# One program order for the whole first pass of a fused attention and gated-FFN kernel, and a shorter float64 rebuild

## Chip, cores and metric

The kernel runs on one core of one Trainium2 chip. The metric is device microseconds (us) of one execution, lower is better.

## Reference

Pooled attention over 8 batches, 8 heads, 576 positions and head size 64, followed by a gated feed-forward layer on the 4608 tokens. Everything is float32.

```python
def _attn_ref(q, k, v):
    k_p = k.reshape(B, H, Sp, pool, D).mean(axis=3)     # pool = 8, Sp = 72
    v_p = v.reshape(B, H, Sp, pool, D).mean(axis=3)
    scores = scale * np.matmul(q, k_p.transpose(0, 1, 3, 2))
    scores = scores - np.max(scores, axis=-1, keepdims=True)
    attn = np.exp(scores)
    attn = attn / (np.sum(attn, axis=-1, keepdims=True) + 1e-09)
    return np.matmul(attn, v_p)

def _moe_ref(x, w_gate, w_val, w_out):                  # 512 -> 1536 -> 512
    gate = 1.0 / (1.0 + np.exp(-(x @ w_gate)))
    return gate * (x @ w_val) @ w_out
```

The three weights arrive as float64; q, k and v as float32.

## The kernel before

The 4608 tokens are cut into 12 blocks of 384. A *pass* takes two blocks: pass n = 0 computes the feed-forward part of blocks 0 and 1, pass 1 that of blocks 2 and 3, up to pass 5. While a pass multiplies, the attention of the next two blocks runs between its products (`both`, `attention`), so pass 0 holds the attention of blocks 0, 1, 2 and 3.

Float32 products are made of three products of rounded parts: each operand is split into a high part (a copy by ACT into a 22-bit type, here called hi) and a low part (the difference, by DVE, lo). `xo` tiles are the parts of an attention result, `parts` those of a weight, `hs` those of the hidden layer, `oparts` those of `w_out`.

Pass 0 differs from the later ones. It has to rebuild each weight as float32 from the two 32-bit words of the float64 value (`to_f32`), split it (`converted`), keep the parts and the whole float32 weight in device memory (`keep`, `kept_w`; DMA issues named `keptG0A`, `keptwG` and so on), and use the parts at once in plain products (`whole`, 12 matmuls for one of G or V, one column group f and one block). There are 12 such weight pieces (G and V, p from 0 to 5; a piece gives f = 2p and 2p + 1). Later passes reload the kept parts and use a seven-product scheme (`product`), for which pass 1 makes sums of the whole weights (`add_up`, tile `w8`, and `sums`). The products of f = 8 to 11 for blocks 2 and 3 are still plain and open pass 1 (`hidden_second`, line 575 of the profile like those of pass 0).

Pass 0 before the change has three stages. `first_blocks` does the attention of blocks 0 and 1 and the first four products, in an order written out by hand (`manual_schedule`, line 1083) for PE, DVE, ACT and POOL. `hidden_first` does the other plain products, converts the remaining eight weight pieces and runs the attention of blocks 2 and 3 in between; its order comes from a scheduler. `second` rebuilds `w_out` (12 pieces, `convert_o`) and multiplies the hidden layer with it (line 717, tile `acc`). All loads and stores are issued by SP, in one queue.

`to_f32` takes one ACT instruction and four DVE instructions:

```python
pinned(nc.scalar.activation(w, hi.bitcast(F32), AF.Abs, scale=2.0 ** -112))             # L122, ACT
nc.vector.tensor_scalar(out=w, in0=w, scalar1=F64_MAX, ...op0=ALU.min)                   # L124, DVE
nc.vector.tensor_scalar(out=u, in0=u, scalar1=3, ...op0=ALU.logical_shift_left)          # L126, DVE
nc.vector.scalar_tensor_tensor(out=u, in0=hi, scalar=0x80000000, in1=u, ...)             # L128, DVE
nc.vector.scalar_tensor_tensor(out=u, in0=lo, scalar=29, in1=u, ...)                     # L132, DVE
```

Pooled v of batch 0 and of batch 1 is made by PE, as a product with a matrix of ones (`v_main`, line 1010, tile `vp`; `v_rest`, line 1020, tile `vr`); of the later batches by DVE reductions (`pool`, line 304, then `prep_v`).

Of the kernel before, what the change touches and what calls it, by code (L numbers as in the profile page):

```python
# [18 lines left out]
P = 128  # L19
# [41 lines left out]
def attention_then_ffn(ctx: ExitStack, tc: tile.TileContext, qT, kT, vm, vr, vn, sums8, wgv, wo, const, out, outT):  # L61
# [54 lines left out]
    words, parts, plain, oparts = {}, {}, {}, {}  # L116

    def to_f32(w, lo, hi):

        u = w.bitcast(U32)  # L120

        pinned(nc.scalar.activation(w, hi.bitcast(F32), AF.Abs, scale=2.0 ** -112))  # L122
# [12 lines left out]
        yield  # L135

    def fetch(kind, p):
        raw = big.tile([P, 4 * HALF, 2], U32, name="raw64", tag="big")
        nc.sync.dma_start(raw.rearrange("p n t -> p (n t)"), wgv[p, "GV".index(kind)].bitcast(U32))
        words[kind, p] = raw  # L140
# [11 lines left out]
    made = [0]  # L152

    def room_for_parts():

        made[0] += 1
        if made[0] <= 4 * NP and made[0] % 11 in (8, 9, 10):
            return work.tile([P, 2, 2, HALF], F32R, name="parts_x", tag=f"xo{(3, 6, 7)[made[0] % 11 - 8]}")
        return wpool.tile([P, 2, 2, HALF], F32R, name="parts", tag="parts")

    def converted(kind, p):
# [4 lines left out]
        w = (big if p else wpool).tile([P, 4, HALF], F32, name="w4", tag="big" if p else "parts")  # L166
        yield from to_f32(w.rearrange("p a n -> p (a n)"), raw[:, :, 0], raw[:, :, 1])
        for i, at in enumerate((slice(0, 4, 3), slice(1, 3))):
# [73 lines left out]
    def convert_o(f):  # L242
        raw = big.tile([P, 3 * DM], U32, name="raw_o", tag="big")
        nc.sync.dma_start(raw[:, :2 * DM], wo[f].bitcast(U32))
        pair = raw[:, :2 * DM].rearrange("p (n t) -> p n t", t=2)
        w = raw[:, 2 * DM:].bitcast(F32)
        for _ in to_f32(w, pair[:, :, 0], pair[:, :, 1]):
            pass
        t = opool.tile([P, 2, DM], F32R, name="oparts")
        split(t[:, 0], t[:, 1], w)  # L250
        nc.sync.dma_start(kept_o[f].rearrange("p h n -> p (h n)").bitcast(F32), t.rearrange("p h n -> p (h n)").bitcast(F32))
        for half in range(2):
# [3 lines left out]
        oparts[f] = t  # L256
# [97 lines left out]
    prepared, xs = {(0, 0), (0, 1)}, {}  # L354
# [17 lines left out]
    def rest_of(e, rz, copy):  # L372
# [11 lines left out]
        copy(r3v[2], restf)  # L384
        return r3

    def attention(j, g):
# [38 lines left out]
        r3 = rest_of(e, rz, nc.scalar.copy)  # L426
# [162 lines left out]

    def hidden_first(tasks):  # L590

        for p in range(1, NP + 1):
            if p in (2, 4):
                new_h(p // 2)
            for i in range(2):
                if p + 1 < NP:
                    steady[0] = p == 1
                    convert("GV"[i], p + 1)
                    steady[0] = False
                if 1 < p < NP:  # L600
# [97 lines left out]

    def second(tasks, build):
        order = ("b0", "b2", "b1", "b4", "b5", "b3")  # L700
        acc = {}
        for f in range(2):
            convert_o(f)
        for f in range(NF):
            if f + 2 < NF:
                convert_o(f + 2)
            hs = big.tile([P, 2, 2 * BT], F32R, name="hs", tag="big")
            hf = hb[f // 4][:, f % 4]
            nc.scalar.copy(hs[:, 0], hf)
            nc.vector.tensor_tensor(out=hs[:, 1], in0=hf, in1=hs[:, 0].bitcast(F32), op=ALU.subtract)  # L710
            o = oparts.pop(f)
            for i in range(2 * QT):
                if f == 0:
                    acc[i] = ps.tile([P, DM], F32, name="acc", tag=order[i])
                a = slice(i * P, (i + 1) * P)
                for k, (y, w) in enumerate(((0, 0), (1, 0), (0, 1))):
                    nc.tensor.matmul(  # L717
                        acc[i], lhsT=hs[:, y, a], rhs=o[:, w], start=(f == 0 and k == 0), stop=(f == NF - 1 and k == 2),
                    )
            if f < 5:  # L720
                next(tasks, None)
                next(tasks, None)
            elif f == 5:
                for _ in tasks:
                    pass
            else:
                next(build, None)
                if f == NF - 1:
                    next(build, None)
        for j in range(2):  # L730
            o = big.tile([P, QT, DM], F32, name="o", tag="big")
            for i in range(QT):
                store(o[:, i], j * BT + i * P, acc[j * QT + i], nc.vector if i % 2 else nc.scalar)
# [147 lines left out]
    def first_blocks():  # L881
# [304 lines left out]
```

## Time and profile before

| | us |
|---|---|
| median of 3 runs | 991.08 (989.36 to 992.35) |
| profiled execution, its own time | 990.34 |
| span of the profiled execution | 988.6 |

The time is that of one execution as the host sees the device; the span is from the first to the last instruction of the trace, and 1.7 us lie around it. Times in the trace count from the start of the span. PE is the matmul engine, DVE and ACT the two elementwise engines, POOL the general one, SP issues the DMAs. [...] A record (xN in the rows) is one instruction as the trace shows it; a float32 score matmul leaves two records.

### The profile page before, as it was taken

Reading aid. Unit: us, or ns where it says so; the run is one execution under the profiler, and the core shown is the slowest. Engines: PE = TensorE matmul, PEld = TensorE weight load, DVE = VectorE, ACT = ScalarE, POOL = GpSimd, SP = SyncE. Lnnn points to the kernel's source line nnn. Section 1 sums busy time; section 2 is a strip of 40 time slices with the busy share of each in tenths; the row PEclk is TensorE's granted clock in tenths of the full one; section 3 lists DMA queues with packets and bytes.
Section 4 is the critical chain, followed back from the end, with each engine's and each line's share of the span. In section 5 each row is a group of like instructions: output and inputs, shape, how many; then the busy total and the mean of one; then the engine's idle time right before and its main releaser. Section 6 shows DMA issues by size and latency. Waiting matters only on the chain.

```text
span 988.6 us, 15480 instructions
## 1 busy us (share of the span) xinstructions
PE 951.3 (96%) x5436; PEld 916.1 (93%) x5436; DVE 709.9 (72%) x1240; ACT 545.0 (55%) x1111; POOL 48.8 (5%) x67
## 2 busy tenths in 40 slices
PE   5779999999899999999999999999999999999998
PEld 4669999889899999998999999999999999999998
DVE  5867799885999789785598666689366669244474
ACT  4647677554576756655455456556355546233343
POOL 2010000000000000000000000000000000000000
PEclk8879999999999999999999999999999999999999
DMA  9736999678799578999558878747976637867567
GB/s 338 256 111 203 342 360 343 225 261 272 237 353 392 187 226 265 315 398 346 180 172 274 279 230 256 235 147 227 309 243 208 224 118 246 292 220 252 181 196 230
DMA packets 114861, 250.84 MB, mean 254 GB/s; under 512 B 11872, under 2 KB 49504, under 8 KB 113248
## 3 DMA queue, kind: packets, MB, share of 16 engines
q1 hardware_dynamic: 114784, 249.86, 75.0%
q8 instruction: 43, 0.70, 0.3%
q14 instruction: 34, 0.28, 0.1%
HBM read 193.19 MB, written 56.62 MB: 253 GB/s over the span
## 4 chain that ended last, share of the span: by engine, by line
PE 84%; DMA 6%; DVE 6%; ACT 3%; issue 1%; SPq 0%; DVEq 0%; ACTq 0%
PE chain L535 38%; PE acc L809 19%; PE chain L575 12%; PE acc L717 5%; PE sc L361 4%; PE av L370 3%; DMA out<-o 1%; PE tp L449 1%; PE vp L1010 1%; DVE s L741 1%; DVE hs L773 1%; DMA parts<-keptV2A 1%; DMA parts<-keptG4B 1%; DMA w<-keptwG 1%; DMA parts<-keptG1B 1%
## 5 line engine op out<-in xcount | busy, mean ns | idle before, releaser
L535 PE MATMUL chain<-xo,parts 128*128 128x384 f32 x2352 | 440.0, 340 | 6.4 <-ACT sV L541 1.5
L535 PEld LDWEIGHTS chain<-xo,parts 128*128 128x128 f32 x2352 | 407.7, 188 | 11.4 <-DVE y L547 2.4
L809 PE MATMUL acc<-hs,oparts 128*128 128x384 f32 x1260 | 229.1, 336 | 3.0 <-DVE hs L773 2.7
L809 PEld LDWEIGHTS acc<-hs,oparts 128*128 128x128 f32 x1260 | 218.3, 188 | 5.4 <-DVE hs L773 3.9
L575 PE MATMUL chain<-xo,parts 128*128 128x384 f32 x552 | 109.3, 351 | 4.5 <-DVE xo L104 2.5
L575 PEld LDWEIGHTS chain<-xo,parts 128*128 128x128 f32 x552 | 100.4, 196 | 6.7 <-DVE xo L104 3.0
L547 DVE TENSOR_TENSOR y<-chain,sG 128x384 f32<-128x384 f32 x84 | 46.3, 552 | 78.1 <-DMA out<-o 25.7
L547 DVE TENSOR_TENSOR y<-chain,sV 128x384 f32<-128x384 f32 x84 | 45.8, 550 | 40.2 <-PE chain L535 24.3
L443 POOL TENSOR_TENSOR pm<-e,rz 128x384 f32<-128x384 f32 x40 | 37.6, 939 | 678.9 <-DVE rz L424 409.4
L541 ACT COPY sG<-chain 128x384 f32<-128x384 f32 x84 | 40.1, 478 | 54.7 <-PE chain L535 54.5
L773 DVE TENSOR_TENSOR hs<-h,hs 128x768 fp32r<-128x768 f32 x60 | 57.4, 961 | 14.8 <-ACT hs L772 14.7
L541 ACT COPY sV<-chain 128x384 f32<-128x384 f32 x84 | 40.1, 477 | 47.0 <-PE chain L535 44.1
L772 ACT CAST hs<-h 128x768 fp32r<-128x768 f32 x60 | 50.1, 835 | 28.6 <-PE acc L809 26.8
L553 ACT ACTIVATE gate<-y 128x384 f32<-128x384 f32 x84 | 43.9, 525 | 38.9 <-DVE y L547 38.4
L772 ACT CAST hs<-s 128x768 fp32r<-128x768 f32 x45 | 36.7, 835 | 31.5 <-PE acc L809 19.6
L717 PE MATMUL acc<-oparts,hs 128*128 128x512 f32 x216 | 52.0, 394 | 0.0
L773 DVE TENSOR_TENSOR hs<-s,hs 128x768 fp32r<-128x768 f32 x45 | 43.6, 980 | 6.6 <-ACT hs L772 6.3
L556 DVE TENSOR_TENSOR h<-y,gate 128x384 f32<-128x384 f32 x84 | 46.8, 561 | 1.6
L717 PEld LDWEIGHTS acc<-oparts,hs 128*128 128x128 f32 x216 | 39.9, 188 | 8.0 <-issue 0.2
L575 PE MATMUL chain<-xo,parts_x 128*128 128x384 f32 x216 | 43.0, 341 | 0.0
L361 PE MATMUL sc<-kbd,raw 128*128 128x144 f32 (+1 forms) x256 | 42.5, 296 | 0.0
L361 PEld LDWEIGHTS sc<-kbd,raw 128*128 128x128 f32 (+1 forms) x256 | 33.7, 177 | 6.7 <-issue 4.6
(168 smaller groups left out, 1186.0 us busy)
## 6 DMA issues: line engine op xcount, KB each, us to landing
oparts<-keptS SPq DMA_DIRECT2D x60, 512.0 KB, 4.5
oparts<-keptO SPq DMA_DIRECT2D x90, 256.0 KB, 3.9
raw<-in_wgv SPq DMA_DIRECT2D x12, 1024.0 KB, 7.6
raw<-in_qT SPq DMA_DIRECT2D x42, 192.0 KB, 4.3
raw<-in_kT SPq DMA_DIRECT2D x28, 288.0 KB, 4.3
out<-o SPq DMA_DIRECT2D x40, 192.0 KB, 4.5
raw<-in_vm SPq DMA_DIRECT2D x24, 256.0 KB, 4.4
raw_o<-in_wo SPq DMA_DIRECT2D x12, 512.0 KB, 4.6
```

What stands on the lines that cost most here:

```text
L361: nc.tensor.matmul(sc[lo - i * P:hi - i * P, i], lhsT=q[:, lo:hi], rhs=kbd[slot(b, p)], start=True, stop=True)
L443: nc.gpsimd.tensor_tensor(out=pm, in0=e[:, n, :, :KM], in1=rz[:, n, :, None].broadcast_to([P, 2 * QT, KM]), op=ALU.mult)
L535: nc.tensor.matmul(t, lhsT=w[:, h, a], rhs=x[:, y, c], start=(m in (1, 2, 5) and c == 0 and k == 0), stop=(c == 1 and k == 2), skip_group_ ...
L541: nc.scalar.copy(s, t)
L547: nc.vector.tensor_tensor(out=y, in0=t, in1=seen[kind, {2: 1, 3: 6, 7: 5}[m]], op=ALU.add)
L553: nc.scalar.activation(gates[q[0]][:, q[1]], y, AF.Sigmoid)
L556: nc.vector.tensor_tensor(out=hb[f // 4][:, f % 4, q[0] * BT:(q[0] + 1) * BT], in0=y, in1=gates[q[0]][:, q[1]], op=ALU.mult)
L575: nc.tensor.matmul(t, lhsT=w[:, c // 2, h, a], rhs=x[:, y, c % 2], start=(c == 0 and k == 0), stop=(c == NC - 1 and k == 2),)
L717: nc.tensor.matmul(acc[i], lhsT=hs[:, y, a], rhs=o[:, w], start=(f == 0 and k == 0), stop=(f == NF - 1 and k == 2),)
L772: nc.scalar.copy(hs[:, 0], x)
L773: nc.vector.tensor_tensor(out=hs[:, 1], in0=x, in1=hs[:, 0].bitcast(F32), op=ALU.subtract)
L809: nc.tensor.matmul(acc[name, c], lhsT=w[:, k, h, c * P:(c + 1) * P], rhs=hs[:, y, k], start=(m in (1, 2, 5) and i % 3 == 0 and k == 0 and ...
```

## The change

Three edits, all in pass 0.

1. **One order.** `first_blocks`, `hidden_first` and `second` are replaced by `first_pass`, which reads a list of about 750 words (`ORDER`, found by a search) and issues one step for each word, in that order, on PE, DVE, ACT, POOL and now SP too (so loads and kept copies stand in the list: `first`, `lk`, `lq`, `lv`, `lr`, `lw`, `ol` are loads, `keep`, `kw`, `keepo`, `keepw` are kept copies). A number behind `@` names the PSUM bank.
2. **A shorter rebuild on DVE.** The low bits of a weight are made by a second ACT instruction (a Relu over the upper 16 bits of the low word, with a bias column `third`), and the shift by 3 moves into a two-input DVE instruction that was there already: two ACT and three DVE instructions instead of one and four.
3. **Pooled v of batch 1 on DVE**, by reductions of separately loaded v (`lv`, `lr`, `vsum`, `rsum`, `vlo`, `rlo`), with the rest's placing on ACT (`vput`); PE's ones product stays for batch 0 alone. The third copy of a small attention part (`rest_again`) goes from DVE to ACT in blocks 0 and 1.

```diff
 def to_f32(w, raw):
     pinned(nc.scalar.activation(w, hi.bitcast(F32), AF.Abs, scale=2.0 ** -112))
     yield
+    half = raw.bitcast(U16).rearrange("p (n t) -> p n t", t=4)[:, :, 1]
+    nc.scalar.activation(lo, half, AF.Relu, scale=2.0 ** -13, bias=third)
+    yield
     nc.vector.tensor_scalar(out=w, in0=w, scalar1=F64_MAX, scalar2=None, op0=ALU.min)
     yield
-    nc.vector.tensor_scalar(out=u, in0=u, scalar1=3, scalar2=None, op0=ALU.logical_shift_left)
-    yield
-    nc.vector.scalar_tensor_tensor(
-        out=u, in0=hi, scalar=0x80000000, in1=u, op0=ALU.bitwise_and, op1=ALU.bitwise_or
-    )
-    yield
-    nc.vector.scalar_tensor_tensor(
-        out=u, in0=lo, scalar=29, in1=u, op0=ALU.logical_shift_right, op1=ALU.bitwise_or
-    )
+    nc.vector.scalar_tensor_tensor(out=lo, in0=hi, scalar=0x80000000, in1=lo, op0=ALU.bitwise_and, op1=ALU.bitwise_or)
+    yield
+    nc.vector.scalar_tensor_tensor(out=u, in0=u, scalar=3, in1=lo, op0=ALU.logical_shift_left, op1=ALU.bitwise_or)
     yield
...
+ORDER = """
+first.0.1 first.0.0 keys.0.0 first.1.1 keys.0.1 put.0.0 put.0.1 sc.0.1@0 lv.1.0 lw.0.0 lk.1.0 vsum.1.0 vhi.1.0
...
+acc.10.1 acc.11.0 out.0 out.1 out.2 st.0 st.2 st.1 acc.11.1 out.3 out.4 st.3 out.5 st.4 st.5
+"""
...
+        engines = (nc.vector, nc.scalar, nc.tensor, nc.gpsimd, nc.sync)
+        with tc.manual_schedule(engines={e.engine for e in engines}):
+            for word in ORDER.split():
+                what, _, named = word.partition("@")
+                tags[:] = [CHAIN[int(i) - 2] if int(i) > 1 else ("sc", "tp")[int(i)] for i in named.split(",") if i]
+                what, *args = what.split(".")
+                does[what](*map(int, args))
...
+        def v_sum(j, p):
+            pool(vs[p], raws["v", j, p], nc.vector)
...
-    first_blocks()
+    first_pass()
...
         if n == 0:
-            hidden_first(tasks)
-        elif n == 1:
+            continue
+        if n == 1:
             hidden_second(tasks)
```

What the list does is seen in the engines' own orders. A row is an instruction: its line, its kind, output <- inputs, shape, and how many follow each other. `chain` is a plain product, `av` and `sc` are attention products (values and scores), `tp` and `tr` turns of attention weights, `_number` a tile's number.

PE, before, around its first plain product: the last values of block 0, three products, then the first scores of block 1 (`kbd4` is the first slot of batch 1).

```order
L370 MATMUL av_422<-early4_218,vl3_104 128x384
L370 MATMUL av_422<-early4_219,vres3_109 128x384
L575 MATMUL chain_469<-xo1_431,parts_434 128x384 x6
L575 MATMUL chain_469<-xo2_460,parts_434 128x384 x6
L575 MATMUL chain_488<-xo1_431,parts_463 128x384 x6
L575 MATMUL chain_488<-xo2_460,parts_463 128x384 x6
L575 MATMUL chain_509<-xo1_431,parts_502 128x384 x6
L575 MATMUL chain_509<-xo2_460,parts_502 128x384 x6
L361 MATMUL sc_522<-kbd0_91,raw_444 128x144
```

PE, of the change, around its first plain product (line 645 is the old 575, 447 the old 370, 438 the old 361): the first values of block 1 and scores of block 3 (`sc_666`, `sc_671`) stand ahead of it.

```order
L447 MATMUL av_632<-ph_232,vl4_105 128x192
L447 MATMUL av_632<-pr_231,vres4_110 128x192
L438 MATMUL sc_666<-kbd4_95,raw_589 128x144 x3
L438 MATMUL sc_671<-kbd3_94,raw_629 128x144 x3
L987 MATMUL tp_682<-cst_87,pm_225 128x128 x3
L645 MATMUL chain_697<-xo1_627,parts_496 128x384 x6
L645 MATMUL chain_697<-xo2_621,parts_496 128x384 x6
L994 MATMUL tr_713<-identr_89,r3_661 96x128 x3
```

The scores of block 1, all of block 0, the scores of block 2 and half of the scores of block 3 have moved ahead of the first plain product; before, only block 0 stood there.

DVE, before, from the second weight piece's rebuild on (`w4_429`); lines 124, 126, 128 and 132 are the four steps of `to_f32`, 172 the low part, 939 a sum of keys.

```order
L104 TENSOR_TENSOR xo2_460<-xs0_406,xo2_460 128x768
L172 TENSOR_TENSOR parts_463<-w4_335,parts_463 128x2x256
L124 TENSOR_SCALAR w4_429<-w4_429 128x1024
L126 TENSOR_SCALAR w4_429<-w4_429 128x1024
L128 SCALAR_TENSOR_TENSOR w4_429<-raw64_237,w4_429 128x1024
L132 SCALAR_TENSOR_TENSOR w4_429<-raw64_237,w4_429 128x1024
```

DVE, of the change, around the two operands of block 0 (`xo2_621`, `xo1_627`, on which the first plain product waits); 198 is the third step of the rebuild, 238 the low part, 1003 the low part of turned weights, 1050 that of v of batch 1, 381 and 966 to 968 sums.

```order
L1086 TENSOR_TENSOR xo2_621<-xs0_221,xo2_621 128x768
L1086 TENSOR_TENSOR xo1_627<-xs0_221,xo1_627 128x768
L1050 TENSOR_TENSOR vl0_101<-small_223,vh0_96 64x64 x2
L198 SCALAR_TENSOR_TENSOR w4_445<-w4_445,raw64_339 128x1024
L1003 TENSOR_TENSOR early4_219<-tp_542,early4_219 128x384
L1003 TENSOR_TENSOR early4_218<-tp_682,early4_218 128x384
L381 TENSOR_REDUCE small_223<-raw_657 128x64
L238 TENSOR_TENSOR parts_371<-w4_262,parts_371 128x2x256
```

The operands of block 0 stood behind 40 rows of DVE before; now they are its 75th and 76th row, and the steps of a weight are spread between attention steps.

SP, before, the first loads; `early<-in_vn` and `in_sums` feed PE's sums of v, `raw64<-in_wgv` is a weight piece of 1.05 MB.

```order
L900 DMA early_216<-in_qT 128x384
L900 DMA early_217<-in_sums8 128x360
L139 DMA raw64_230<-in_wgv 128x2048
L900 DMA early_216<-in_vn 128x512 x3
L900 DMA early_217<-in_vn 128x512
L900 DMA h_220<-in_vn 64x512
L139 DMA raw64_237<-in_wgv 128x2048
L139 DMA raw64_239<-in_wgv 128x2048
L139 DMA raw64_241<-in_wgv 128x2048
L925 DMA early_216<-in_vn 128x512 x2
```

SP, of the change, its first loads; `in_vm` and `in_vr` are v of batch 1 for DVE.

```order
L880 DMA early_216<-in_qT 128x384
L368 DMA raw_249<-in_vm 128x512
L203 DMA raw64_251<-in_wgv 128x2048
L361 DMA raw_253<-in_kT 128x576
L880 DMA early_216<-in_qT 128x384
L880 DMA h_220<-in_kT 128x576
L372 DMA raw_267<-in_vr 32x512 x3
L364 DMA raw_271<-in_qT 128x384
```

Four weight pieces followed each other within the first seventeen issues; now one stands in the fifth and the next in the fourteenth row, with keys, queries and v of batch 1 between.

## Rows read from the trace of the kernel before

**Rows 1.** The page, parts 1 and 2: engines, then tenths in 40 slices.

```profile
PE 951.3 (96%) x5436; PEld 916.1 (93%) x5436; DVE 709.9 (72%) x1240; ACT 545.0 (55%) x1111; POOL 48.8 (5%) x67
...
PE   5779999999899999999999999999999999999998
...
PEclk8879999999999999999999999999999999999999
```

**Rows 2.** Windows by stage: window, length, busy (records), clock, DMA share, GB/s.

```profile
0.00:90.00 90.00, 68.00 (x331) 58.45 (x332) 59.96 (x108) 51.24 (x141) 11.22 (x27) 0.83 0.64 228
90.00:231.00 141.00, 141.00 (x765) 130.77 (x764) 121.59 (x209) 90.04 (x187) 7.98 (x8) 1.00 0.87 299
335.00:988.60 653.60, 640.80 (x3741) 627.48 (x3739) 438.71 (x736) 336.80 (x640) 24.33 (x27) 1.00 0.72 238
```

**Rows 3.** Four short windows of the same view (PE, PEld, DVE, ACT, POOL, clock, DMA).

```profile
10.00:20.00 10.00, 6.54 (x28) 4.96 (x28) 8.69 (x18) 8.06 (x31) 3.16 (x4) 0.69 1.03 388
70.00:80.00 10.00, 8.76 (x41) 8.39 (x42) 6.46 (x15) 5.79 (x13) 0.88 (x2) 0.57 0.28 107
110.00:120.00 10.00, 10.00 (x62) 9.96 (x61) 7.34 (x12) 7.91 (x16) 0.00 (x0) 1.00 0.94 321
250.00:255.00 5.00, 5.00 (x22) 5.00 (x23) 4.48 (x9) 3.15 (x5) 0.00 (x0) 0.73 0.45 152
```

**Rows 4.** The chain that ended last, in order of time: start, us, what.

```profile
1.19 3.19 DMA h<-in_kT
...
7.17 3.22 PE sc L361 x12
...
50.95 3.41 PE vp L1010 x8
...
231.50 5.56 DMA w<-keptwG
```

**Rows 5.** PE groups by form, 0 to 90 us: xcount, busy us, mean ns.

```profile
L575 PE MATMUL chain<-xo,parts 128*128 128x384 f32 x119 | 27.1, 384 | 2.0 <-ACT parts L170 1.8
L1010 PE MATMUL vp<-early 128*128 128x256 f32 x32 | 10.4, 490 | 0.0
```

**Rows 6.** DVE groups by form, 0 to 231 us.

```profile
L132 DVE SCALAR_TENSOR_TENSOR w<-raw,w 128x1024 uint32<-128x1024 uint32 x12 | 15.1, 1262 | 0.1
L128 DVE SCALAR_TENSOR_TENSOR w<-raw,w 128x1024 uint32<-128x1024 uint32 x12 | 14.6, 1215 | 0.2
L172 DVE TENSOR_TENSOR parts<-w,parts 128x512 fp32r<-128x512 f32 x18 | 12.5, 715 | 0.9 <-ACT parts L170 0.7
L126 DVE TENSOR_SCALAR w<-w 128x1024 uint32<-128x1024 uint32 x12 | 8.4, 701 | 0.1
L126 DVE TENSOR_SCALAR raw_o<-raw_o 128x512 uint32<-128x512 uint32 x12 | 5.1, 421 | 0.2
L304 DVE TENSOR_REDUCE vs<-raw 128x64 f32<-128x512 f32 x6 | 4.1, 680 | 2.9 <-DMA raw<-in_vm 2.9
```

**Rows 7.** ACT groups by form, 0 to 231 us.

```profile
L122 ACT ACTIVATE w<-raw 128x1024 f32<-128x1024 f32 x12 | 13.8, 1148 | 3.9 <-DMA raw<-in_wgv 3.9
L122 ACT ACTIVATE raw_o<-raw_o 128x512 f32<-128x512 f32 x12 | 8.0, 669 | 9.8 <-DMA raw_o<-in_wo 7.0 <-DVE rz L424 2.7
L420 ACT ACT_TABLE_LOAD x6 | 7.7, 1283 | 1.1 <-DVE m L408 1.0
L583 ACT ACT_TABLE_LOAD x5 | 6.4, 1283 | 0.1
```

**Rows 8.** Start of pass 1: PE's waits from 225 to 300 us, DVE's timeline.

```profile
PE chain L575 <- DVE xo L104: 2.5, 1, 2.5
...
230.65 0.68 DVE L694 COPY o<-acc 128x512 f32<-128x512 f32 x1
237.08 0.69 DVE L188 TENSOR_TENSOR w<-w 128x512 f32<-128x512 f32 x1 [5.76 <-DMA w<-keptwG]
```

**Rows 9.** Windows again: pass 0 in four stages (DVE, ACT, DMA).

```profile
0.00:31.00 31.00, 17.83 (x82) 14.34 (x82) 19.03 (x40) 16.54 (x53) 6.48 (x23) 0.89 0.92 328
90.00:176.00 86.00, 86.00 (x510) 85.75 (x509) 78.22 (x133) 60.90 (x129) 4.71 (x5) 1.00 0.94 331
sum 231.00, PE 209.00 PEld 189.22 DVE 181.56 ACT 141.28 POOL 19.20; mean PE 52.25 PEld 47.31 DVE 45.39 ACT 35.32 POOL 4.80
```

More of the change, by code (lines that the diff above doesn't have):

```diff
@@ L697, in store @@
         nc.sync.dma_start(out[r:r + P], o)
[L699 to L733, printed above, removed]
     s1 = {}
@@ new lines, in first_pass, with of_e @@
+        vrc = [other["V5"][:96, D * g:D * g + D] for g in range(2)]
+        prs = [work.tile([96, BT], F32R, name="pr"), x5[:96, 0], other["V1"][:96]]
+        phs = [work.tile([P, BT], F32R, name="ph"), x5[:, 1], x4[:, 0], x4[:, 1], other["G5"]]
+        pls = [work.tile([P, BT], F32R, name="pl"), x5[:, 2], x4[:, 2], x4[:, 3], other["G6"]]
+        scs, rests, av, vp, raws, conv, ygate, vbank, hss, acc, outs = ({} for _ in range(11))
+        tags = []
+        def of_e(j, p):
+            return es[p // 2 if j < 2 else 0]
@@ L1075, in first_blocks, with x_hi, x_lo @@
-        conv = {}
-        def c(kind, p, n=1):
+            if j > 1 and sum(k[0] == j for k in waiting) == PAIRS:
+                xs[j % 2] = work.tile([P, NC, BT], F32, name=f"xs{j % 2}")
+            nc.scalar.copy(xs[j % 2][:, p], av[j, p])
+        def x_hi(j, h):
+            m = ((1, 2), (5, 4))[j % 2][h]
+            xo[m] = work.tile([P, 2, NC // 2, BT], F32R, name=f"xo{m}", tag=f"xo{m}")
+            nc.scalar.copy(xo[m][:, 0], xs[j % 2][:, 2 * h:2 * h + 2])
+        def x_lo(j, h):
+            t = xo[((1, 2), (5, 4))[j % 2][h]]
+            nc.vector.tensor_tensor(
+                out=t[:, 1], in0=xs[j % 2][:, 2 * h:2 * h + 2], in1=t[:, 0].bitcast(F32), op=ALU.subtract
+            )
@@ L1113, in first_blocks, with step_o, product_g, product_v @@
-        for t in conv.values():
-            for _ in t:
-                pass
-        prepared.update((1, g) for g in range(2))
-        held[0] = False
-    first_blocks()
+            next(conv[kind, p])
+        def step_o(f):
+            if f not in conv:
+                conv[f] = converted_o(f)
+            next(conv[f])
+        def product_g(j, f):
+            vbank["G", j, f] = whole("G", f, j, tags.pop(0))
+        def product_v(j, f):
+            vbank["V", j, f] = whole("V", f, j, tags.pop(0))
@@ new lines, in hs_lo, with accumulate @@
+        def hs_lo(f):
+            nc.vector.tensor_tensor(
+                out=hss[f][:, 1], in0=hb[f // 4][:, f % 4], in1=hss[f][:, 0].bitcast(F32), op=ALU.subtract
+            )
+        def accumulate(f, half):
+            for i in range(QT * half, QT * half + QT):
+                if f == 0:
+                    acc[i] = bank_for([P, DM], "acc")
+                a = slice(i * P, (i + 1) * P)
+                for k, (y, w) in enumerate(((0, 0), (1, 0), (0, 1))):
+                    nc.tensor.matmul(
+                        acc[i], lhsT=hss[f][:, y, a], rhs=oparts[f][:, w], start=(f == 0 and k == 0),
+                        stop=(f == NF - 1 and k == 2),
+                    )
```

507 lines of the change are left out of this document (267 added, 240 removed), and 4 rows, old and new, of the table banks.

## Prediction

> **What bounds the kernel now.** I read the page first: over the whole span PE is busy 96%, DVE 72%, ACT 55%, and PE's digits are below 9 only in the first three slices and the last [rows 1]. So a gain has to come from PE's time, and most of what PE lacks lies at the start. The windows by stage size it. From 335 us on PE is busy 640.8 of 653.6 us: 12.8 us are open in two thirds of the span. From 90 to 231 us it has no gap: 765 records in 141.0 us. In the first 90 us only 331 records run, at a mean granted clock of 0.83 [rows 2]. A dense stretch does 62 records in 10 us, 0.161 us each [rows 3]; 331 would take 53.3 us, so about 37 us of the first 90 are waits and slow clock. [...]
>
> What PE waits for there is no single engine: DVE is busy 59.96 and ACT 51.24 of the 90 us [rows 2], and the chain passes between keys' DMA, PE's scores and PE's ones products for v of batch 1 [rows 4]. PE does 32 matmuls `vp` (10.4 us) in this stretch, half of them for batch 1, and 119 plain products at a mean of 384 ns [rows 5]. The plain products of a short beginning soon run out of operands; block 1's attention then proceeds with little beside it. Pass 0 ends at about 231 us: the last eviction of `acc` starts at 230.65 [rows 8].
>
> **The change: the new beginning.** The list trades an early first product for a dense remainder: all the scores that the first blocks need, and some of the next, come before it. I counted in the orders what stands ahead of the first plain product: 170 records on PE, 80 DVE instructions (through `xlo` of block 0) and 119 on ACT. Each engine's own work bounds its time from below:
>
> - DVE: 59.96 us over 108 instructions is 0.555 each [rows 2]; 80 of them are 44.4 us, and nothing can start before the first keys land at 1.19 + 3.19 = 4.38 us [rows 4]: 48.8.
> - ACT: 51.24/141 = 0.363 [rows 2]; 119 x 0.363 + 4.4 = 47.6.
> - PE: its scores start at 7.17 [rows 4]; 170 x 0.161 at the clock of 0.69 [rows 3] is 39.7, so 46.9; wholly at the lower level, twice 0.161, it is 62.0.
>
> Three engines with nearly equal sums that hand to each other can't all be dense. DVE's share, after the first keys, is 19.03 of 26.6 us = 0.715 in 0 to 31 [rows 9], and 0.87 in 10 to 20 us [rows 3]. The new list has several heads and two batches to draw on where the old had one, so I take 0.87: 44.4/0.87 + 4.4 = **55.4 us**; bounds 48.8 (dense) and 44.4/0.715 + 4.4 = 66.5 (as now).
>
> **The rest of pass 0.** Records: 331 + 765 = 1096 now [rows 2]. Off go PE's v sums of batch 1, 24 by the order (16 `vp`, 8 `vr`); on come 14 of block 3's last two pairs (8 values, 6 turns) which now run after 231 us. That is 1086, of which 916 stand behind the first 170. 765 of them are the work of the 141.0 us; the other 151, mostly plain products, cost 0.161 each if dense [rows 3], 24.4 us (at the 0.228 that 27.1/119 gives now [rows 5] it would be 34.4). With 1.0 us, a choice, for products begun at the lower clock the pass ends at 55.4 + 141.0 + 24.4 + 1.0 = **221.8** in place of 231: 9.2 us earlier. The 14 records are missing behind it: 2.3 us more.
>
> Can DVE feed that? Its pass-0 sum is 181.56 now [rows 9]. The shift by 3 that goes is 12 x 0.701 + 12 x 0.421 = 13.5; six reductions at 0.680 come, 4.1 (the nearest row [rows 6]), and about 2.5 of block 3, for which I scale the 14 records' 2.3 us: 174.7. After the first product that leaves 130.3 in 166.4 us, a share of 0.78. The stage 90 to 176 held 78.22/86 = 0.91 with PE full [rows 9], so the forecast does not ask DVE for more than it does now. The two-input steps now read the raw words in other places; nearest rows 1.215 and 1.262, upper bound 1.43 (twice the 0.715 of the half-sized subtraction [rows 6]). Below 1.215 nothing is excluded, the raw operand being read in both. I take 1.24; the upper end adds 2 x 12 x 0.2 = 4.8 us spread over the pass, of which the three weights ahead of the first product carry 1.2.
>
> ACT gets 24 Relus over 16-bit words. The Abs beside them takes 1.148 and 0.669 [rows 7]; the same price gives 12 x 1.817 = 21.8, bounds half and twice that. ACT then has 141.28 + 21.8 = 163.1 in 222 us, 0.73; at twice 184.9, 0.83, still below what DVE bears. Hidden by PE, it costs nothing; were it not, three weights ahead of the first product would add 3.4 us. Table loads cost 1.283 each (11 in two lines now [rows 7]); five more or fewer are 6.4 us of ACT, within the same slack.
>
> The kept copies and loads in SP's order move the same 62.7 MB in pass 0 (228 x 90 + 299 x 141 us [rows 2]); by 221.8 us that asks 283 GB/s against 271 now. The dense stage moves 331 at a share of 0.94 [rows 9], and 10 to 20 us 388 [rows 3]: I cost it at nothing, with a rival below. `vput` and the third copy on ACT, POOL's part (19.20 us of 231 [rows 9]) and later passes I cost at nothing as well; later swaps of order can move the 12.8 open us by perhaps 1.5 either way.
>
> **Hand-over to pass 1.** Now PE waits 2.5 us for `xo` of block 3 [rows 8] and runs 22 records where 31 fit in 250 to 255 us at a clock of 0.73 [rows 3], 1.5 more: 4.0 lost. That wait goes, since block 3 is done within the pass. Late next is the sum `w8`: its weight load starts at 231.50 behind the output stores on SP and takes 5.56 us [rows 4], DVE waits 5.76 for it [rows 8], and the list leaves that load behind the stores, with 2.3 us less plain work to cover DVE's sums. I take the loss as unchanged, 0; bounds -4.0 (all gone) and +2.3 (the shorter cover returned).
>
> **Sum.** -9.2 - 2.3 + 0 = -11.5. Profiled 990.34 - 11.5 = 978.8, the span 1.7 less. The profiled execution is 0.7 below the median of 991.08, so the forecast for a median is **979.5**.
>
> **Rivals** (each with the same 166.4 us behind its first product, and 0.7 for the median).
>
> [...]
> - *The beginning is dense.* DVE at its 48.8: the pass ends at 215.2, time 973.0, with a hand-over that loses nothing 969.0. For it: every wait of the first 90 us is one of order. Against: DVE has no more than 0.87 in 10 to 20 us [rows 3], the stretch with most DMA.
> - *No change.* DVE's share remains 0.715, the first product is at 66.5, the pass ends at 232.9: 990.7. For it: sparse attention waits by hand-overs, which an order can't remove. Against: far more independent work is in the list there.
> - *Slower: the queue.* Everything issues in one strict order, SP as well; a kept copy waiting for its parts holds every load behind it, and a late load then holds all engines. If the queue's mean falls to the middle of 228 and 299 [rows 2], 263.5 GB/s, 62.7 MB take 238.0 us, and the time is 995.8. It decides below 62.7 MB / 236.3 us = 265 GB/s. For it: only 271 is shown over pass 0. Against: that mean holds stretches at 107 GB/s [rows 3] which had little to load, and 331 was sustained for 86 us.
>
> **Numbers.** Forecast 0.60, low clock 0.14, dense 0.13, no change 0.06, queue 0.07. About 0.3% (3 us) is what a measurement of this kernel can tell from no change. Faster: 0.60 + 0.14 + 0.13 = 0.87; same 0.06; slower 0.07. The forecast's own range, from a first product between 52 and 59 us and the hand-over's bounds, is 972 to 985. The range that also takes in the dense and the low-clock case is 965 to 989, the lower end 4 us below the dense one, for the price of the 151 records and of the later orders.
>
> **What would show it.** First plain product (line 645) near 55 us (49 dense, 62 low clock, 66 as now); PE without gaps from there to a last `acc` near 222; DVE at about 0.78 between, its steps 196 and 198 near 1.24 us; Relu rows (192) near 1.15 and 0.67; no wait of DVE or ACT for weight loads; at the start of pass 1 no wait for `xo` of block 3, but some 4 us for `w8`. I am wrong if PE has gaps of several us after its first product (the list then has a wait I did not see), if the first product comes late by more than 60, or if gains of the beginning return as a longer opening of pass 1.

## The result and the profile after

The changed kernel takes 978.12 us (median of 4, 976.57 to 979.58) against 991.72 beside it; the ratio is 0.9866 (0.9842 to 0.9891). The profiled execution took 978.66 us with a span of 976.9, so 11.7 us of span went. Single executions of the kernel before spread over 1% (984.4 to 993.9 in one set of 17), so a stage read from one profile is no better than some 1.5 us: a second profile of the changed kernel ended pass 0 at 223.8 in place of 222.3.

The page of the changed kernel, engines and slices, answers to [rows 1]:

```profile
PE 940.9 (96%) x5412; PEld 906.5 (93%) x5412; DVE 700.8 (72%) x1221; ACT 553.6 (57%) x1138; POOL 51.8 (5%) x67
...
PE   4789999999999999999999999999999999999998
...
PEclk9999999999999999999999999999999999999999
```

Its windows, with columns as in [rows 2] (the clock is the one granted to TensorE, as a share of its full speed): the first 90 us, the beginning up to the first plain product, the rest of pass 0, the opening of pass 1 (up to the first seven-product row), the rest of pass 1:

```profile
0.00:90.00 90.00, 67.83 (x384) 59.50 (x385) 75.88 (x139) 71.39 (x193) 15.29 (x31) 0.98 0.91 312
...
0.00:51.80 51.80, 31.74 (x171) 25.37 (x171) 40.00 (x77) 39.18 (x124) 10.59 (x27) 0.97 0.92 309
51.80:222.70 170.90, 167.83 (x916) 156.35 (x914) 132.29 (x222) 113.27 (x232) 9.83 (x8) 1.00 0.78 271
222.70:256.50 33.80, 33.80 (x199) 33.11 (x198) 24.94 (x52) 14.65 (x29) 0.15 (x1) 1.00 0.87 295
256.50:384.00 127.50, 125.71 (x753) 122.83 (x753) 116.98 (x218) 83.30 (x173) 10.46 (x9) 1.00 0.82 281
```

In the first 90 us PE is idle as long as before (22.2 us against 22.0, [rows 2]), but runs 384 records in place of 331, at a clock of 0.98 in place of 0.83; DVE and ACT are busy 16 and 20 us more. Its waits there:

```profile
PE sc L438 <- ACT kbd L948: 8.4, 1, 8.4
PE tp L987 <- POOL pm L971: 2.5, 3, 1.5
PE sc L438 <- DMA raw<-in_qT: 2.5, 3, 1.2
```

The opening of pass 1 against the same piece of the kernel before, by its windows:

```profile
231.00:271.50 40.50, 37.98 (x211) 37.19 (x211) 31.72 (x63) 20.51 (x37) 0.83 (x1) 0.96 0.77 251
271.50:395.80 124.30, 124.30 (x757) 122.80 (x756) 112.89 (x211) 82.40 (x172) 9.25 (x9) 1.00 0.82 284
```

It is 6.7 us shorter: 12 records fewer, no wait (2.5 before), a clock of 1.00 (0.96 before). The rest of pass 1 is 3.2 us longer. So the 11.7 us are 8.3 at the end of pass 0, 6.7 in the opening, and 3.3 given back behind it.

The new instructions cost, on DVE (lines 196, 198) and on ACT (192) up to 223 us:

```profile
L196 DVE SCALAR_TENSOR_TENSOR raw<-raw 128x1024 uint32<-128x1024 uint32 x12 | 14.7, 1228 | 0.0
L198 DVE SCALAR_TENSOR_TENSOR w<-w,raw 128x1024 uint32<-128x1024 uint32 x12 | 14.6, 1213 | 0.1
```

```profile
L192 ACT ACTIVATE raw<-raw,cst 128x1024 uint32<-128x1024 uint16 x12 | 15.1, 1255 | 0.1
...
L192 ACT ACTIVATE raw_o<-raw_o,cst 128x512 uint32<-128x512 uint16 x12 | 9.2, 769 | 0.0
```

### The profile page after: what moved, and what is told of

Read it like the earlier page. It is cut to its first block, busy times and chain, and to the rows that moved or that the text cites. A ratio compares the mean times of both kernels' runs of the same rounds, so it can differ in the third digit from the quotient of the medians.

```text
span 976.9 us, 15387 instructions
## 1 busy us (share of the span) xinstructions
PE 940.9 (96%) x5412; PEld 906.5 (93%) x5412; DVE 700.8 (72%) x1221; ACT 553.6 (57%) x1138; POOL 51.8 (5%) x67
## 4 chain that ended last, share of the span: by engine, by line
PE 71%; DVE 13%; DMA 10%; ACT 4%; issue 2%; SPq 1%; POOL 0%; DVEq 0%; POOLq 0%; ACTq 0%
PE chain L605 35%; PE acc L825 18%; PE chain L645 7%; PE acc L1133 5%; PE av L447 2%; PE sc L438 2%; DMA raw<-in_kT 1%; DVE hs L789 1%; DVE s L757 1%; DMA raw_o<-in_wo 1%; DMA w<-keptwO 1%; DMA w<-keptwV 1%; PE tp L526 1%; DMA raw<-in_wgv 1%; DMA keptwV<-w 1%
## 5 line engine op out<-in xcount | busy, mean ns | idle before, releaser
L520 POOL TENSOR_TENSOR pm<-e,rz 128x384 f32<-128x384 f32 x32 | 31.3, 979 | 601.9 <-DVE rz L500 347.2
L438 PE MATMUL sc<-kbd,raw 128*128 128x144 f32 (+1 forms) x280 | 47.6, 306 | 3.4 <-DMA raw<-in_qT 2.5
L1133 PE MATMUL acc<-oparts,hs 128*128 128x512 f32 x216 | 50.7, 391 | 0.0
L438 PEld LDWEIGHTS sc<-kbd,raw 128*128 128x128 f32 (+1 forms) x280 | 37.3, 184 | 11.3 <-issue 4.0
L645 PE MATMUL chain<-xo,parts_x 128*128 128x384 f32 x216 | 40.2, 337 | 0.0
```

The source lines that it names most:

```text
L438: nc.tensor.matmul(sc[lo - i * P:hi - i * P, i], lhsT=q[:, lo:hi], rhs=kbd[slot(b, p)], start=True, stop=True)
L520: nc.gpsimd.tensor_tensor(out=pm, in0=e[:, n, :, :KM], in1=rz[:, n, :, None].broadcast_to([P, 2 * QT, KM]), op=ALU.mult)
L645: nc.tensor.matmul(t, lhsT=w[:, c // 2, h, a], rhs=x[:, y, c % 2], start=(c == 0 and k == 0), stop=(c == NC - 1 and k == 2),)
L1133: nc.tensor.matmul(acc[i], lhsT=hss[f][:, y, a], rhs=oparts[f][:, w], start=(f == 0 and k == 0), stop=(f == NF - 1 and k == 2),)
```

## The experiments

Three sets of four, each set timed against the kernel before on its own chip. The table has the ratio with its 95% interval and, from the line views of each profile, when PE starts its first plain product, its last `w_out` product of pass 0, its first seven-product row, its last `w_out` product of pass 1, and how long passes 2 to 5 take from there to the last product.

| kernel | ratio | first plain | end pass 0 | first seven | end pass 1 | passes 2 to 5 |
|---|---|---|---|---|---|---|
| before | 1 | 31.3 | 230.6 | 271.5 | 395.7 | 589.2 |
| the change | 0.9866 (0.9842 to 0.9891) | 51.8 | 222.3 | 256.5 | 383.9 | 589.3 |
| after_again | 0.988 (0.9853 to 0.9908) | 51.5 | 223.8 | 257.9 | 385.4 | 587.8 |
| filled | 0.9992 (0.997 to 1.0014) | 32.3 | 229.9 | 269.2 | 393.7 | 588.9 |
| relu_alone | 1.008 (1.0052 to 1.0108) | 31.7 | 234.9 | 274.8 | 403.4 | 586.1 |
| order_alone | 1.0002 (0.9983 to 1.002) | 54.0 | 227.0 | 261.3 | 388.3 | 594.8 |
| shift_back | 0.9962 (0.9939 to 0.9984) | 52.8 | 224.1 | 258.5 | 385.1 | 593.4 |
| gv_pe | 0.9973 (0.9952 to 0.9994) | 51.7 | 224.1 | 258.3 | 386.6 | 590.6 |
| shift_gv | 0.9927 (0.9903 to 0.9951) | 52.8 | 227.0 | 261.2 | 388.6 | 587.9 |
| shift_o | 0.9899 (0.9875 to 0.9923) | 51.9 | 221.1 | 255.4 | 381.9 | 592.4 |
| no_min | 0.9882 (0.9862 to 0.9902) | 49.5 | 221.4 | 255.6 | 382.7 | 588.8 |
| min_pool | 0.9889 (0.9864 to 0.9914) | 50.7 | 221.5 | 255.6 | 383.2 | 589.6 |
| late_parts | 0.9913 (0.989 to 0.9937) | 51.4 | 223.0 | 257.4 | 386.9 | 592.9 |
| more_dma | 0.9927 (0.9907 to 0.9946) | 50.8 | 224.3 | 258.5 | 386.1 | 588.6 |

A profile shows one execution. That of gv_pe is one of its fastest (982.98 us, median 986.3), that of more_dma its fastest (980.02, median 983.56), and those of relu_alone and shift_back lie 2.1 and 2.3 us under their medians; that of late_parts lies 3.4 us over its median (985.31, 981.96). Over the whole span their stages are off by as much.

### filled: is it the clock?

The kernel before, where PE repeats work just ahead of two waits:

```diff
-        for c in range(NC):
+        for c in [c for _ in range(2 if (kind, f, side) == ("V", 1, 0) else 1) for c in range(NC)]:
...
-            av_matmuls(av[j, p], phs[p], pls[p], prs[p // 2], segments(j), p)
+            for _ in range(3 if (j, p) == (1, 0) else 1):
+                av_matmuls(av[j, p], phs[p], pls[p], prs[p // 2], segments(j), p)
```

> The kernel before, with PE kept busy in two of its waits by repeating work with the same result: the plain product V1 of block 0 twice (12 records more, ahead of the wait of 2.66 us near 46 us) and the values of batch 1's first pair three times (16 records more, ahead of the wait of 3.0 us near 67 us). Theory 'clock': behind each of these two waits the granted clock stands at 0.50 for 7 and 10 us, in which PE is busy about 15 us; kept busy, PE keeps the clock at 1.00 there, pass 0 ends about 5 to 7 us earlier, ratio to before 0.993 to 0.995. Theory 'operands' (the prediction's own): PE waits for DVE, ACT and POOL in those stretches, a faster PE only waits longer; the end of pass 0 stays within 1 us, ratio 0.999 to 1.003.

Its windows, and those of the kernel before:

```profile
0.00:90.00 90.00, 71.22 (x370) 62.25 (x371) 62.08 (x109) 53.06 (x144) 11.14 (x27) 0.94 0.65 230
46.00:56.00 10.00, 9.43 (x55) 7.73 (x54) 9.83 (x17) 7.63 (x28) 2.29 (x2) 1.00 0.54 193
68.00:80.00 12.00, 10.32 (x55) 10.11 (x56) 6.55 (x15) 6.27 (x14) 0.96 (x2) 0.72 0.33 126
```

```profile
46.00:56.00 10.00, 7.36 (x27) 5.42 (x28) 8.37 (x13) 6.87 (x23) 2.29 (x2) 0.66 0.46 166
68.00:80.00 12.00, 8.76 (x41) 8.39 (x42) 8.40 (x17) 5.79 (x13) 2.45 (x2) 0.57 0.24 89
```

The clock rose as meant, from 0.66 to 1.00 and from 0.57 to 0.72, and 0.83 to 0.94 over 90 us; the time did not move (0.9992). What PE gains in clock it waits for operands, as the theory "operands" had it (3.2 us for `parts` in the first 100 us, where it was 1.8). So in the kernel before these higher clocks by themselves are worth nothing. That the change's clock (0.98) only goes along with its gain is inferred from this; no run lowers the clock in the new order.

### relu_alone: the second edit in the kernel before

The kernel before with the new `to_f32` (diff in the section on the change) and its bias column.

> The kernel before with the second edit alone (two ACT and three DVE instructions for a rebuild, in the old order). Theory 'order': DVE's 13.5 us are mostly beside PE's dense stretch; in the first 90 us four weight pieces save 4 x 0.70 = 2.8 us of DVE, of which 1 to 2 us reach the end of pass 0; ratio to before 0.998 to 0.999. Rival 'rebuild': DVE sets the end of pass 0 and the rebuild is where the change gains; 6 us or more earlier, ratio below 0.994.

Both theories miss: it is 0.8% slower. Its windows:

```profile
0.00:90.00 90.00, 66.27 (x328) 57.30 (x329) 58.23 (x104) 56.51 (x146) 10.97 (x27) 0.89 0.66 231
90.00:176.00 86.00, 85.11 (x504) 84.55 (x503) 69.35 (x114) 66.64 (x129) 3.85 (x4) 1.00 0.93 324
176.00:234.90 58.90, 57.81 (x261) 45.71 (x260) 42.91 (x74) 37.87 (x77) 2.49 (x3) 1.00 0.68 238
```

DVE falls by 11 us over pass 0 against [rows 9], ACT rises by 20, PE is dense no longer from 90 us on and pass 0 ends 4.3 us later. But the old order was kept only as far as it is written out by hand. Up to 80.8 us (81.0 in relu_alone) PE's records are the same in both kernels, so the shorter rebuild had gained nothing by then; from there on the scheduler wrote another order, in the rest of pass 0 and behind it. The run does not part the edit from that order. The longer chain through two ACT steps fits (ACT waits 6.9 us for DVE's rebuilt weights in pass 0, 4.8 before), but it is not shown to be the reason.

### order_alone and shift_back: the order without its relief

shift_back takes the second edit back in the new list; order_alone also puts PE records of the third edit's size back, ahead of batch 1's scores:

```diff
-        nc.scalar.activation(lo, half, AF.Relu, scale=2.0 ** -13, bias=third)
+        nc.vector.tensor_scalar(out=lo, in0=lo, scalar1=29, scalar2=None, op0=ALU.logical_shift_right)
...
             scs[j, p] = bank_for([P, QT, 2 * KEYS], "sc")
+            if j == 1:
+                t = scs[j, p].rearrange("p i k -> p (i k)")
+                for _ in range(2):
+                    nc.tensor.matmul(t[:, :256], lhsT=q[:, :P], rhs=q[:, :256], start=True, stop=True)
+                nc.tensor.matmul(t[:96, :P], lhsT=q[:D, :96], rhs=q[:D, :P], start=True, stop=True)
```

> The changed kernel with the second edit taken back (the Relu on ACT becomes a shift on DVE, 0.70 us, in the same place of the list) and with the PE work that the third edit removed put back as 24 extra PE records ahead of batch 1's scores. So the new order without its relief. Theory 'order': first plain product 2 to 3 us later (three shifts), end of pass 0 at 225 to 226, ratio to before 0.989 to 0.991. Rival 'relief' (less DVE and PE work is what pays): 13.5 us of DVE and 5 us of PE come back, the ratio is above 0.996.

> The changed kernel with only the second edit taken back (shift on DVE in the Relu's place). Theory 'order': DVE goes from 0.77 to 0.85 of the time behind the first plain product, which PE's queue of products still covers; first product 2.1 us later, end of pass 0 2 to 3 us later (225), ratio to before 0.988 to 0.990. Rival 'DVE bound': most of the 13.5 us come back, end of pass 0 near 233, ratio near 0.998.

As it stands, the new order without the reliefs gains nothing (1.0002). This refutes the theory "order", which was the prediction's view of where the gain comes from. But the table shows two things in it: pass 0 ends 3.6 us earlier than before and the first seven-product row comes 10.2 us earlier, and then passes 2 to 5 take 594.8 and 593.4 us where the change takes 589.3. Nothing in those passes was edited. From pass 1 on a scheduler writes the order, and it writes another one for these two kernels: PE's rows differ from the change's in 65 places. (The list also sets SP's order; no run separates that part from the engines' orders.)

### after_again, shift_gv, gv_pe, shift_o: the same with the later order held

With the shift on DVE only for the 12 gate and value pieces (the diff; in shift_o the condition is the width `DM`, and gv_pe adds the PE records shown above) the scheduler writes PE's later order as in the change, row for row; with the shift only for the `w_out` pieces it writes that of shift_back. That separates the two.

```diff
+        if w.shape[1] == 4 * HALF:
+            nc.vector.tensor_scalar(out=lo, in0=lo, scalar1=29, scalar2=None, op0=ALU.logical_shift_right)
+        else:
+            nc.scalar.activation(lo, half, AF.Relu, scale=2.0 ** -13, bias=third)
```

> The changed kernel itself, beside the next three on one chip: ratio to before 0.984 to 0.989, last matmul of pass 0 near 222, passes 2 to 5 near 589 us.

> The changed kernel with the shift back on DVE for the 12 gate and value pieces alone (8.4 us more DVE, 15 us less ACT); PE's order behind pass 0 is the changed kernel's, row for row. Theory 'two parts': of the 1.0% between shift_back and the change, pass 0 holds 1.8 us, and 4 to 5 us come from the order that the scheduler writes for the later passes, which differs between those two kernels in 65 places on PE. Then pass 0 ends 1 to 2 us later than in the change, passes 2 to 5 take 589 us as there, ratio to before 0.988 to 0.990. Rival 'relief': the rebuild's DVE time itself is worth 9 us; ratio 0.994 or more.

> As shift_gv, with the 24 PE records of the third edit put back ahead of batch 1's scores too, so nearly the new order alone, with the changed kernel's later passes. 'Two parts': end of pass 0 at 226 to 227 (3 us for the PE records), passes 2 to 5 at 589, ratio 0.990 to 0.993: the order alone then gains 7 to 10 us. Rival 'relief': as order_alone, 0.999 or more.

> The changed kernel with the shift back on DVE for the 12 pieces of w_out alone (5 us more DVE, in the part of pass 0 where DVE is half idle, 9 us less ACT). For the later passes the scheduler writes the order that shift_back and order_alone have. 'Two parts': pass 0 ends within 0.5 us of the change's, but passes 1 to 5 are 4 to 5 us longer, ratio 0.990 to 0.992. Rival: the later order is worth nothing; ratio as the change's, 0.986 to 0.987.

In the column of passes 2 to 5, the kernels with the change's PE order there have 587.8 to 590.6 us, the four with the other 592.4 to 594.8: the scheduler's side effect is some 4.5 us. With it held, the ratios part the gain: nearly the order alone (gv_pe, which keeps the Relu for `w_out` and batch 1's v sums on DVE) 0.9973, that is 2.7 us of 989; without the 24 PE records 0.9927, 4.5 us more (order_alone against shift_back gives 4.0); with DVE's 12 shifts gone 0.988, 4.6 us more. The intervals leave each of these uncertain by some 3 us, but "relief" is nearer than my "two parts" for both kernels. The profiles bear out the last step alone: shift_gv ends pass 0 3.2 us later than after_again. They do not show where the 24 records cost their time (gv_pe's pass 0 ends 2.9 us ahead of shift_gv's), and shift_back, with twice as many shifts on DVE as shift_gv, ends pass 0 2.9 us ahead of it. shift_o lies between its two expectations; its own pass 0 ended early, at 221.1.

Where the 8.4 us of DVE come in is seen from 80 to 150 us. Two windows of the change, then one each of shift_gv, gv_pe, and before:

```profile
80.00:150.00 70.00, 69.99 (x412) 69.55 (x412) 67.72 (x117) 58.11 (x126) 6.42 (x5) 1.00 0.99 348
150.00:222.00 72.00, 71.03 (x345) 61.81 (x344) 38.50 (x61) 31.91 (x52) 0.00 (x0) 1.00 0.53 181
```

```profile
80.00:150.00 70.00, 68.51 (x396) 66.14 (x395) 67.01 (x111) 49.72 (x116) 7.10 (x6) 1.00 0.97 339
```

```profile
80.00:150.00 70.00, 68.01 (x392) 65.80 (x391) 67.00 (x112) 49.08 (x116) 5.12 (x4) 1.00 0.95 330
```

```profile
80.00:150.00 70.00, 70.00 (x421) 69.79 (x421) 61.03 (x96) 49.21 (x104) 3.65 (x4) 1.00 0.90 316
```

DVE is busy 0.97 there in the new order, 0.87 in the old. With the shift back it is as full, and does 5 or 6 instructions fewer in the 70 us; PE, dense in the change, idles 1.5 to 2.0 us and runs 16 to 20 records fewer, some 3 us. PE's waits from 52 to 160 us show for whom, first in the change, then in shift_gv (`y` is the gate, by ACT; `h` the hidden layer, by DVE):

```profile
PE chain L645 <- ACT y L1109: 1.0, 1, 1.0
```

```profile
PE chain L651 <- ACT y L1115: 1.7, 1, 1.7
...
PE chain L651 <- DVE h L1120: 1.3, 2, 0.9
```

Both kernels have the same records on PE, so their starts can be compared one by one: shift_gv is 0.9 us behind the change at 103 us, 3.1 at 135 and 4.8 at 160 (the second profile of the change: 1.0, 1.0 and 1.6). So with the shift back DVE sets the pace in this stretch. In the change it is full there while PE is just dense, though over all of 51.8 to 222.7 us its share is 132.29/170.9 = 0.77.

### no_min and min_pool: still less for DVE

no_min first, min_pool behind the dots:

```diff
-        nc.vector.tensor_scalar(out=w, in0=w, scalar1=F64_MAX, scalar2=None, op0=ALU.min)
+        if w.shape[1] == DM:
+            nc.vector.tensor_scalar(out=w, in0=w, scalar1=F64_MAX, scalar2=None, op0=ALU.min)
...
+        rebuilt[0] += 1
+        (nc.gpsimd if w.shape[1] > DM and rebuilt[0] > 3 else nc.vector).tensor_scalar(out=w, in0=w, scalar1=F64_MAX, scalar2=None, op0=ALU.min)
```

> The changed kernel without the clamp (min, 0.685 us on DVE) of the 12 gate and value pieces, which leaves out the bound for weights that overflow float32: DVE is relieved by 8.2 us more; later passes in the changed kernel's order. Theory 'DVE dense': from 52 to 150 us DVE is busy 0.95 and sets PE's pace, so that part of the relief arrives that lies ahead of the first product or where PE still idles: first product 1 to 2 us earlier, pass 0 ends 2 to 4 us earlier, ratio to before 0.983 to 0.986. Rival 'average share' (the prediction's: DVE at 0.78 has room): end of pass 0 within 1 us of the change's, ratio 0.987 to 0.988.

> The changed kernel with that clamp on POOL for the gate and value pieces from the fourth rebuild on (9 of 12, 6.2 us off DVE, nothing left out). By POOL's row for 128 x 384 (0.98 us) a piece takes about 2.6 us there, so each rebuild is some 2 us longer from end to end. Theory 'DVE dense': pass 0 ends 1 to 3 us earlier if the rebuilds are ahead of need; ratio 0.984 to 0.987. Rival 'latency': the longer rebuild holds ACT and DVE, which run in strict order behind it, by 2 us for each of 9 pieces; ratio 0.992 or more.

The first product comes 2.3 us earlier without the clamps, and DVE's share from 80 to 150 us falls to 0.87, but the ratio is the change's (0.9882): the rival's value, by another mechanism than the rival's. The window, and PE's and ACT's longest wait from 80 and 60 to 160 us:

```profile
80.00:150.00 70.00, 68.30 (x402) 67.77 (x400) 60.77 (x109) 56.32 (x125) 5.12 (x4) 1.00 0.99 353
...
PE chain L646 <- ACT y L1110: 1.9, 1, 1.9
...
ACT raw_o L188 <- DMA raw_o<-in_wo: 4.8, 1, 4.8
```

ACT waits for the load of a `w_out` piece (in the change 5.6 us in two waits), its gates behind that come late, and PE waits for a gate. In order of time, the load's issue, ACT and PE:

```profile
142.27 0.45 SPq L312 DMA_DIRECT2D raw_o<-in_wo  x1
...
147.73 0.66 ACT L188 ACTIVATE raw_o<-raw_o 128x512 f32<-128x512 f32 x1 [4.79 <-DMA raw_o<-in_wo]
...
150.20 3.08 PE L646 MATMUL chain<-xo,parts 128*128 128x384 f32 x12 [1.90 <-ACT y L1110]
```

By PE's records no_min is 3.7 us ahead of the change before this wait and 1.2 us ahead behind it. So with DVE relieved the next limit stands close behind: a load that comes late. Whether the DMA queue makes it late (its share is 0.99) or its place in SP's list, these rows do not separate. min_pool, with nothing left out, is no faster either (0.9889); a clamp of 128 x 1024 took 3.21 us on POOL, and what that and the longer rebuild cost is within the noise.

```profile
L197 POOL TENSOR_SCALAR w<-w 128x1024 f32<-128x1024 f32 x9 | 28.9, 3212 | 16.0 <-ACT w L190 16.0
```

### late_parts: the hand-over

```diff
-rcopy.3.1 acc.5.0 av.3.2@6 x.3.2 hslo.7 av.3.3@1 acc.5.1 acc.6.0 x.3.3 xhi.3.1 xlo.3.1 oconv.9
+rcopy.3.1 acc.5.0 av.3.2@6 x.3.2 hslo.7 av.3.3@1 acc.5.1 acc.6.0 x.3.3 oconv.9
...
-st.3 out.5 st.4 st.5
+st.3 out.5 st.4 st.5 xhi.3.1 xlo.3.1
```

> The changed kernel with the parts of the second half of block 3's attention result (an ACT and a DVE instruction) moved behind the last output copies of pass 0, where the kernel before had that step; the later passes then come in shift_o's order. Theory 'hand-over': PE waits again at the start of pass 1, the stretch from the last product of pass 0 to the first seven-product grows from 34.2 us by 3 to 4, and the end of pass 1 is as much later; ratio 0.993. Rival 'absorbed': the wait comes back, but pass 1 has that much room, its last w_out product stays 161 to 162 us behind the end of pass 0, ratio as shift_o, 0.989 to 0.991.

The wait did not come back: from the end of pass 0 to the first seven-product row it is 34.4 us (34.2 in the change), so the place of that one step was not what the old opening lost. The rest of pass 1 is 2 us longer, in an execution 3.4 us over the median; PE's longest wait from 215 us to 340 is one of 1.9 us for a kept part. Neither theory stands as put; which of the moved pieces of block 3 (14 PE records, the evictions, the parts) held PE before stays open.

### more_dma: how much the queue has left

```diff
     def fetch(kind, p):
+        if kind == "G" and 1 <= p <= 4:
+            nc.sync.dma_start(dram.tile([P, 8 * HALF], U32, name=f"copy{p}"), wgv[p, 0].bitcast(U32))
```

> The changed kernel with four copies more of a weight piece within device memory (4 x 1.05 MB read and written, nobody reads the copies) issued in SP's order ahead of the gate pieces 1 to 4. Theory 'queue near its bound': the DMA share is 0.92 to 0.99 from 0 to 150 us, so 4.2 MB at 331 GB/s, 12.7 us of the queue, delay the loads behind them; pass 0 ends 6 to 13 us later, ratio 0.994 to 1.000. Rival 'slack': the loads run ahead of need, end of pass 0 within 2 us, ratio 0.986 to 0.990.

Windows of the first 150 us, of the change and of more_dma:

```profile
0.00:150.00 150.00, 127.83 (x737) 119.33 (x738) 133.71 (x237) 119.95 (x303) 20.42 (x35) 0.99 0.95 327
```

```profile
0.00:150.00 150.00, 130.72 (x746) 121.66 (x747) 133.15 (x235) 119.69 (x303) 20.41 (x35) 0.98 1.00 355
```

The ratio is 0.9927 against 0.9866 and 0.988 of the change: 4.6 to 6 us for 12.7 us of queue (an estimate: 4.2 MB at the 331 GB/s of [rows 9]). Between the theories: the queue has some slack, but about 40% of what is added arrives. The loads of `w_out` come late first: ACT waits 8.4 us for them from 60 to 160 us (5.6 in the change), and PE 2.8 us for a gate behind them (1.0 in the change):

```profile
ACT raw_o L188 <- DMA raw_o<-in_wo: 8.4, 2, 4.6
...
PE chain L647 <- ACT y L1111: 2.8, 1, 2.8
```

## Why the prediction was right, and where its steps were not

**Sum.** Forecast -11.5 us and 979.5; the profile shows -11.7 and the median is 978.1. The terms were -9.2 (end of pass 0), -2.3 (records gone from behind it) and 0 (hand-over); measured are -8.3 at the end of pass 0 and -3.4 behind it. Two pairs of misses cancel, the beginning against the rest of pass 0 and the opening of pass 1 against its rest; that the sum is this near is partly luck.

**The new beginning.** First product at 51.8 where I had 55.4. The counts were nearly right (171 records on PE, 77 DVE and 124 ACT instructions ahead of it, for 170, 80 and 119); the price per DVE instruction was too high: 40.00 us over 77 is 0.519, not 0.555. With 0.519 the step's own formula gives 52.1. The 0.87 taken for DVE's share was near: 40.00 of 47.4 us after the first keys is 0.84.

**The rest of pass 0.** 170.9 us in place of 166.4. The count was right (916 records); they took 167.83/916 = 0.183 us where the sum had (141.0 + 24.4)/916 = 0.181, 2.4 us more, and PE was idle 3.1 us where I gave 1.0 in all.

**DVE has room: the step that failed.** "The forecast does not ask DVE for more than it does now" rested on a share of 0.78 over 166 us. The share came out as said, and says nothing: it is 0.97 from 80 to 150 us and 0.53 behind that. In the first of these stretches 8.4 us more of DVE cost 4.6 us (shift_gv), which I had costed at nothing beyond the first product; 8.2 us less gained nothing that shows (no_min, where a late load takes the lead back). The gain that I put down to the order is one of order and relief together: the order with most of the reliefs taken back brings 2.7 us (0.6 to 4.7 by its interval). The relief alone has no clean run: put into the kernel before it came with another order and was 0.8% slower.

**PE's 24 records** were priced at 24 x 0.161 = 3.9 us within the count; put back they cost 4.0 and 4.5 by the ratios, each uncertain by some 3 us.

**Hand-over.** Taken as 0 with -4.0 as one bound. The opening lost nothing (-6.7, of which 2.3 was in the sum already), so the bound was the better value; the expected wait of PE for `w8` did not come, though DVE waited 5.4 us for its load. 3.2 us of it are given back within pass 1, where PE idles 1.8 us and was dense before.

**Prices.** The two-input steps 1.228 and 1.213, taken 1.24. Relu 1.255 and 0.769, above the taken 1.148 and 0.669; ACT was busy 58.11 of 70 us from 80 to 150 and 31.91 of 72 behind that, so it had room. The sign "no wait of DVE or ACT for weight loads" did not hold: up to 222.7 us ACT waited 16.4 us for loads of `w_out`, though PE was busy 69.99 of 70 us from 80 to 150.

**Rivals.** Low clock (PE's 62.0, every record at twice 0.161): not so, 0.97 in the beginning with PE busy 31.74 of 51.8 us. No run shows a beginning wholly at such a clock, for which the forecast gave 0.14 and took its range up to 989; the kernel before shows short stretches alone (0.50 from 32 to 36 us, where PE, without a gap, ran 12 records, 0.333 us each). And filled shows that there a clock of 0.94 over the first 90 us, in place of 0.83, leaves the time as it was (0.9992). Dense: not reached, the first product is 3.0 us behind its 48.8, and just below the 52 to 59 that the forecast's own range took. Queue: it moved (309 x 51.8 + 271 x 170.9)/222.7 = 280 GB/s over pass 0, above the 265 at which it would have turned the sign, but it has little left in the first 150 us (327 GB/s at a share of 0.95; more_dma moved 355 at 1.00, with a ratio of 0.9927). No change: order_alone has its time, a case I had not considered, but not its mechanism, since the first product came at 54.0 and not at 66.5.

## What to carry to other kernels

A share of busy time over a long stage can hide a part where the engine is full; cut the window until the share stops changing before an engine is called free. A reordering can be worth little without the relief that comes with it (2.7 us here of some 12), so undo the parts one by one inside the changed kernel, not only in the old one. Where a scheduler orders a part of the program, an edit can move stages that it never touches, here by 4.5 us, more than a third of the whole gain: compare stage by stage and order by order, and pick undo variants for which the other order stays.

## What was not expected of the hardware

PE was idle for 22 us of the first 90 in both kernels, yet the granted clock was 0.83 in one and 0.98 in the other; the sum of the idle time does not give the clock. In the kernel before, the clock was 0.66 from 46 to 56 us and 0.57 from 68 to 80 us, with waits of 2.7 and 3.0 us in them. But it also stood at 0.50 from 14 to 20 and from 32 to 36 us, where PE's waits were 1.8 us at most, and in the change, whose waits behind the first are at most 2.4 us, there is a short dip (0.50 from 32 to 34 us, 0.68 in the next two), while behind the first one, of 8.4 us, the clock was 1.00 up to 30 us. Rows of the kernel before (two), of the change, and of the change's second profile, which had the same median (978.13):

```profile
14.00:16.00 2.00, 0.98 (x5) 0.64 (x5) 1.84 (x6) 1.30 (x7) 1.24 (x2) 0.50 1.13 314
32.00:34.00 2.00, 2.00 (x6) 1.61 (x7) 1.42 (x3) 2.00 (x3) 0.00 (x0) 0.50 0.54 201
```

```profile
32.00:34.00 2.00, 2.00 (x10) 1.34 (x9) 1.93 (x5) 1.94 (x6) 0.63 (x1) 0.50 1.01 325
```

```profile
52.00:80.00 28.00, 26.69 (x152) 26.39 (x153) 24.59 (x44) 21.12 (x53) 2.38 (x3) 0.88 0.85 302
```

What brings the clock down in these stretches stays open. In filled, with 28 more records, it was 1.00 from 46 to 56 us and 0.72 from 68 to 80 us.

A clamp of 128 x 1024 float32 on POOL took 3.21 us (min_pool, mean of nine) against 0.685 on DVE (the change, mean of twelve).
